# Attention and two feed-forward stages: a second transposition for the upper keys, scatters in pairs, row stores from ScalarE's queue

## The chip, the cores and the metric

The kernel runs on one core of one Trainium2 chip. The metric is the device time of one launch in microseconds; the numbers are medians of runs, and the profile is one execution of its own. TensorE (PE) multiplies matrices and transposes, VectorE (DVE) and ScalarE (ACT) work on elements, GpSimd (POOL) too, and it issues the indirect DMAs; SP only issues DMAs, and ACT issues DMAs besides its own work.

## The reference

```python
# attention, B=8, H=8, S=576, D=64; keys and values are means over 8 neighbours (72 of each)
k_p = k.reshape(B, H, 72, 8, D).mean(axis=3)
v_p = v.reshape(B, H, 72, 8, D).mean(axis=3)
scores = np.matmul(q, k_p.transpose(0, 1, 3, 2)) / np.sqrt(D)
attn = np.exp(scores - scores.max(-1, keepdims=True))
attn_out = np.matmul(attn / (attn.sum(-1, keepdims=True) + 1e-09), v_p)
x = attn_out.transpose(0, 2, 1, 3).reshape(4608, 512)
# one of eight experts for each row, by the largest of eight gate values
e_idx = np.argmax(x @ w_gate + modality_bias[modality_id], axis=1)
out[mask] = gate_w[mask, None] * (np.maximum(x[mask] @ w1[e], 0.0) @ w2[e])
# a second feed-forward stage over all rows
h = out @ w_in
solu = h * softmax(h)
y = (layer_norm(solu) * g_ln) @ w_out
```

## The kernel before

All matrices are float32. The weights of the feed-forward stages are held as a high and a low part, so that each product is three matmuls (lines 735 to 737).

**Attention** fills the first 200 us or so. The 64 pairs of batch and head are worked on batch by batch. The keys and the values of a batch are 8 heads x 72 pooled rows = 576 rows, in five row blocks of 128, 128, 128, 120 and 72 rows (`ROWS`). For each block `load_kv` loads a tile `kc` of keys and one `vc` of values (L267). `kv_a` (L328) pools them: the keys by a VectorE reduction (`pool_k`, L302) into `kv[:, 0]`, the values into `kv[:, 1]`, for the first 19 blocks on VectorE (L340), for the others by three additions on GpSimd (L345 to L347). `kv_b` (L353) transposes `kv`, keys and values side by side, in one TensorE transposition for each block (L359): the keys come out on partitions 0 to 63 and the values on 64 to 127. `kv_e` (L362) copies them out of PSUM on ScalarE: the keys into `kb[0:64, 0]` (L369), the values into `vt` (L372).

The scores of two rows of queries are made in one matmul: `kb` has the keys twice, once in its lower partitions and plane 0, once in the upper partitions and plane 1, since the query tile holds one query row in each half. For the first batch `first_keys` (L306) writes both halves; for the others the upper half comes by a DMA from the lower half, L371, on ScalarE's queue, once for a batch when its last block is there. `kv_c` and `kv_d` multiply the pooled values with the gate's weights and build `vb`, whose columns are the values and the gate's share of them (L383, L396, L399).

A **unit** is up to 256 query rows of one batch, or the last 64 rows of two batches; there are 20. For a unit `st_q` transposes queries (L422), the scores are made (L452 for the shared units, L456), VectorE takes a maximum (L466), ScalarE the exponentials (L490), TensorE transposes them back (L503, L506), ScalarE copies them (L516, L518), and `st_v` multiplies them with `vb` (L545). `st_w` (L553) then divides by the sum on VectorE, makes the row block `xr` of 128 rows (L570) and the gate's values (L573, L576), and stores the rows to `xs` in DRAM by a DMA on SP (L577), 36 in all.

Nine row blocks at a time are **routed**: `route` finds the expert, `rank` (L607) counts each row's place in its expert's list with small matmuls (L617, L619), and `scatter` (L632) writes each row's place, weight and token into the list `perm` by an indirect DMA on GpSimd, one for each of the nine blocks (L640). When 18 blocks have been written, `choose` (L664) takes the expert with the most rows; its weights are loaded, its list is read and its rows are gathered from `xs` (L702), as the first slot of the feed-forward part. The table `FIRST` says how many steps after the choice each of these comes.

The order of the work is written as a list of parts, `ORDER`, which each step runs through with lags in units; a scheduler then sets each engine's order. In a step "a" is `kv_a`, "b" `kv_b`, "k" `kv_e`, "c" `kv_c`, "d" `kv_d`, "w" `st_w`, "r" `rank` and "z" `scatter`. After attention come the decoding of `w_in` and `w_out` and, from 307 us, the slots of 256 rows.

Of the kernel before, what the change touches and what calls it, by code (L numbers as in the profile page):

```python
# [37 lines left out]
# which groups of a unit's scores have their maximum taken off on VectorE  # L38
SUBG = ((2,),) * 20
# after which of the first values the second unit's queries are loaded  # L40
# [3 lines left out]
# the row blocks (five to a batch) whose values are pooled on VectorE, not GpSimd  # L44
# [3 lines left out]
# the first slot's loads, by steps since its expert was chosen  # L48
FIRST = {
    1: (("1", 0),),  # L50
    2: (("i", 0), ("g", 0), ("s", 0)),
# [3 lines left out]
    6: (("t", 0),),  # L55
# [3 lines left out]
# a step's parts: what, which, and how many units ahead of the step  # L59
# [9 lines left out]
# the last pair's tiles that are routed together  # L69
# [10 lines left out]
def chunk_attention_moe_solu_kernel(  # L80
# [79 lines left out]
    def fixed_load(src, n, i, *_):  # L160
        kk, cc = divmod(i, n // 512)
        # before the first slot's exponentials their place serves too
        in_ec = (i if n > 512 else 8 + i) in EC
        st = ec_p.tile([128, FF], F32, name="ec") if in_ec else stg_p.tile([128, 1024], F32, name="stg")
        rows = src[128 * kk:128 * kk + 128, 512 * cc:512 * cc + 512]
        if src.dtype != I64:
            SY.dma_start(out=st[:, 0:512], in_=rows)
        else:
            SY.dma_start(out=st.bitcast(I32), in_=rows.bitcast(I32))
        return st  # L170

    def fixed_chunk(st, src, n, i, hi, lo, scale=None):
        """Chunk i (512 columns) of a [rows, n] weight, rows 128 to a partition block, as hi + lo."""
# [6 lines left out]
        else:  # L180
# [5 lines left out]
            # the high word read as a float32 orders magnitudes too: below float32's range they become 0  # L186
# [24 lines left out]
    def expert_load(src, e, kk, n):  # L211
        """Rows of expert e's weight for n of its row blocks of 128, 1024 floats to a partition."""
        st = stg_p.tile([128, 1024], F32, name="stg")
        SY.dma_start(
            out=st.rearrange("p (k f) -> p k f", k=n),
            in_=src[bass.ds(e, 1), 128 * kk:128 * (kk + n), :].rearrange("a (k p) f -> p (a k) f", p=128))
        return st
# [6 lines left out]
    def behind(op, other):  # L224
        """Keeps op behind an earlier one of its engine."""
        tc.add_manual_dep(op.ins, other.ins.name, mybir.DependencyInfo(mybir.DependencyClass.NoSync, mybir.DependencyReason.DATA))
# [71 lines left out]
    # a batch's pooled keys and values in three groups of its five row blocks  # L298
# [7 lines left out]
    def first_keys():  # L306
        """The first batch's pooled keys, ahead of its values."""
# [7 lines left out]
        for b, cs in KG[:3]:  # L315
            a0, z0 = ROWS[cs[0]][0], ROWS[cs[-1]][1]
            kt = pstr.tile([128, 512], F32, name="tr")
            for c in cs:
                a, z = ROWS[c]
                kv = kx_p.tile([128, 2, D], F32, name="kv")  # L320
                pool_k(kv, k_t.pop((b, c)), z - a)
                PE.transpose(out=kt[0:64, a - a0:z - a0], in_=kv[:z - a, 0], identity=ident[:z - a, :z - a])
                PE.matmul(out=kt[64:128, a - a0:z - a0], lhsT=kv[:z - a, 0], rhs=ident[:z - a, :z - a], start=True, stop=True)
                kv_0.append(kv)
# [3 lines left out]
    def kv_a(i):  # L328
        b, cs = KG[i]
        kv_st[i] = []  # L330
        for c in cs:
            n = ROWS[c][1] - ROWS[c][0]
            vc = v_t.pop((b, c))
            if b == 0:
                kv = kv_0[c]
            else:
                kv = kx_p.tile([128, 2, D], F32, name="kv")
                pool_k(kv, k_t.pop((b, c)), n)
            if 5 * b + c in VD:
# [8 lines left out]
            if b == 0 and op is not None:  # L348
                # the keys are waited for first
                behind(op, kv_last[-1])  # L350
            kv_st[i].append(kv)

    def kv_b(i):  # L353
# [3 lines left out]
        for c, kv in zip(cs, kv_st[i]):  # L357
            a, z = ROWS[c]
            PE.transpose(out=kt[:, a - a0:z - a0], in_=kv[:z - a].rearrange("p a d -> p (a d)"), identity=ident[:z - a, :z - a])  # L359
        kv_kt[i] = kt  # L360

    def kv_e(i):  # L362
# [7 lines left out]
        if b and cs[-1] == 4:  # L370
            ACT.dma_start(out=kb[64:128, 1, :], in_=kb[0:64, 0, :])  # L371
# [31 lines left out]
    # units: five per pair of batches (b, k0) (b, k1) (the last 64 tokens of both) (b+1, k0) (b+1, k1)  # L403
# [27 lines left out]
    # scores of a unit in three banks of (up to) six blocks of 72: block i is head i//n of row r = i%n  # L431
    # (in the unit of two batches' ends: head i)
# [89 lines left out]
    def group(i):  # L522
        """The tiles that are routed together: a pair of batches' nine, of the last pair five and four."""
# [4 lines left out]
    # heads' 73 columns follow each other over two banks: seven of them end at the first one's end  # L528
    def st_v(u, r):
# [5 lines left out]
        if not ps2 and s_done.get(NU - 1) == 3 and not any(x[0] == "s" for x in ps):  # L535
            # no more scores: their banks hold every other tile of the last units
# [16 lines left out]
    def st_w(u, r):  # L553
# [23 lines left out]
        SY.dma_start(out=xs[128 * i:128 * i + 128, :], in_=x)  # L577
# [29 lines left out]
    def rank():  # L607
# [8 lines left out]
        # row p of tile j: earlier rows of its tile, and all of the tiles before it  # L616
# [10 lines left out]
        DVE.tensor_copy(out=pi[:, 0:n], in_=pf[:, 0:n])  # L627
        pending.append([g0, pi, n, 0])

    pending = []  # L630

    def scatter(now=False):  # L632
        if not pending:
            return
        if pending[0][3] < 0 and not now:
            pending[0][3] += 1
            return
        g0, pi, n, _ = pending.pop(0)
        for j in range(n):
# [16 lines left out]
    def pick_first(dst, val, tmp, mx):  # L656
        """dst = one-hot of the first largest of val, over the last axis of 8."""
# [6 lines left out]
    def choose():  # L664
        """The expert with most tokens so far, of 18 tiles, has more than SLOT: its first two slots go first."""
# [48 lines left out]
    def take(pool, shape, dt, name):  # L714
        """A tile: a new one, or, in the last slot's two branches, the next of those that both hold."""
# [40 lines left out]
    # the first slot's first stages go between the last units' parts  # L756
# [45 lines left out]
    def more_loads():  # L802
# [14 lines left out]
        # a row's place in xs and its token  # L817
# [31 lines left out]
    for it in range(IT0, NU - min(lag for _, _, lag in ORDER)):  # L849
# [20 lines left out]
        if first is None and len(scatters) >= 18:  # L870
            choose()
            first = it
        for op, x in FIRST.get(it - first, ()) if first is not None else ():
            if op == "i":
                ids0 = id_p.tile([128, 2, 3], I32, name="ids")
# [56 lines left out]
    def tables(tp):  # L932
# [23 lines left out]
        # the expert that goes last: the one with fewest rows in its last slot  # L956
# [35 lines left out]
        # rows left from a slot's start; its first row; its expert (an empty slot has the first one's)  # L992
# [68 lines left out]
    def st_S(s, t, pf):  # L1061
        """Off with the mean; the sum of squares."""
# [7 lines left out]
    def st_R(s, t, n):  # L1070
        """Rows' scale: r / sqrt(r^2 mean(c^2) + 1e-6) with r = 1 / (sum + 1e-9)."""
# [7 lines left out]
        # 1 / sqrt: a first value from the bits, then Newton's steps  # L1079
# [51 lines left out]
    def switch_regs(s):  # L1131
        """Whether slot s needs another expert's weights, which, and its first row."""
# [16 lines left out]
    def switch_split(ce, sts, dh, dl, n, pool=(), after=()):  # L1149
        with tc.If(ce[0] == 1):  # L1150
            for i in range(4):
                ops = expert_split(sts[i], flat(dh[:, n * i:n * i + n]), flat(dl[:, n * i:n * i + n]), POO if i in pool else DVE)
                if i == 0:
                    # behind what the tensor engine waits for
# [22 lines left out]
    for s in range(NSTAT - 1):  # L1177
# [8 lines left out]
        if s > 1:  # L1186
            # behind what the tensor engine waits for
# [209 lines left out]
```

## Time and profile before

| what | value |
| --- | --- |
| median of 3 runs | 1095.69 us |
| lowest and highest run | 1093.2 and 1097.76 us |
| span of the profiled execution | 1114.2 us |
| mean granted TensorE clock in it | 0.981 |
| TensorE busy | 1060.4 us (95%) |
| VectorE busy | 573.9 us (52%) |
| ScalarE busy | 403.9 us (36%) |
| GpSimd busy | 218.2 us (20%) |

No time of the profiled execution other than its span is recorded. The shares are means over stages with different limits, so they are to be read by stage. A duration of a matmul in the rows is from its issue to its modelled end, and successive ones overlap.

### The profile page before, as it was taken

To read this page: it belongs to the slowest core of one execution; us is meant where nothing else is said; L and a number is where in the kernel's file an instruction comes from. 1 tells how busy PE (TensorE), PEld (TensorE's weight loads), DVE (VectorE), ACT (ScalarE), POOL (GpSimd) and SP (SyncE) were. 2 spreads that over 40 slices of the span, in tenths; PEclk is the share of its full clock that TensorE was granted. 3 is DMA by queue.
4 is the path that set the end of the run, shared out by engine and by line. 5 is a ranking of instruction groups with operands and counts; after the bars stand their busy time and mean duration, and the time that the engine had idled before them with its cause. 6 is when DMAs were issued, how large, how long until landed. Compare 5 with 4: busy or idle time off the path is not lost.

```text
span 1114.2 us, 18506 instructions
## 1 busy us (share of the span) xinstructions
PE 1060.4 (95%) x6961; PEld 963.0 (86%) x6961; DVE 573.9 (52%) x1460; ACT 403.9 (36%) x870; POOL 218.2 (20%) x284
## 2 busy tenths in 40 slices
PE   5898979789999999999999999999999999999997
PEld 4788868788889899898998989999898998989875
DVE  7986757899953434333444433434335343333254
ACT  3666657444522322222234222322234222222232
POOL 3147453453420101101013010100121011010001
PEclk8999989989999999999999999999999999999999
DMA  9887856332200101001033010101221010010000
GB/s 254 222 243 216 242 170 213 107 115 96 77 30 11 38 1 39 29 11 39 1 115 100 15 39 2 37 8 32 97 93 39 1 39 26 8 39 2 19 19 32
DMA packets 58960, 81.19 MB, mean 73 GB/s; under 512 B 16670, under 2 KB 33054, under 8 KB 58848
## 3 DMA queue, kind: packets, MB, share of 16 engines
q1 hardware_dynamic: 50608, 59.28, 17.7%
q0 software_dynamic: 7152, 19.46, 5.1%
q10 hardware_dynamic: 1088, 1.05, 0.4%
q8 instruction: 59, 0.97, 0.4%
q14 instruction: 53, 0.43, 0.1%
HBM read 59.37 MB, written 19.63 MB: 71 GB/s over the span
## 4 chain that ended last, share of the span: by engine, by line
PE 62%; issue 10%; DVE 1%; POOL 1%; another core or an unknown queue 0%; POOLq 0%; ACT 0%
PE ab L736 15%; PE ab L735 15%; PE ab L737 15%; PE h L736 5%; PE h L735 5%; PE h L737 5%; PE tr L1101 2%; PE tr L728 1%; POOL out_dram L1120 1%; DVE ta L208 0%; DVE hl L752 0%; DVE ec L1067 0%; DVE ec L1054 0%; DVE c L1077 0%
## 5 line engine op out<-in xcount | busy, mean ns | idle before, releaser
L1120 POOL DMA_INDIRECT out_dram<-o,ids x37 | 37.7, 1019 | 683.0 <-ACT o L1119 557.9
L735 PE MATMUL ab<-hh,w2h 128*128 128x256 f32 x576 | 165.9, 288 | 3.7 <-DVE rpf L626 3.7
L737 PE MATMUL ab<-hh,w2l 128*128 128x256 f32 x576 | 163.7, 284 | 0.0
L736 PE MATMUL ab<-hl,w2h 128*128 128x256 f32 x576 | 163.2, 283 | 0.5 <-DVE hl L752 0.5
L735 PE MATMUL ab<-xh,w1h 128*128 128x256 f32 x544 | 154.6, 284 | 2.9 <-DVE hl L752 1.8
L736 PE MATMUL ab<-xl,w1h 128*128 128x256 f32 x544 | 154.3, 284 | 0.0
L737 PE MATMUL ab<-xh,w1l 128*128 128x256 f32 x544 | 153.5, 282 | 0.0
L736 PE MATMUL h<-wil,yh 128*128 128x512 f32 x296 | 116.4, 393 | 1.9 <-POOL wil L202 1.9
L735 PE MATMUL h<-wih,yh 128*128 128x512 f32 x296 | 117.9, 398 | 0.1
L737 PE MATMUL h<-wih,yl 128*128 128x512 f32 x296 | 116.0, 392 | 0.0
L735 PEld LDWEIGHTS ab<-hh,w2h 128*128 128x128 f32 x576 | 109.9, 191 | 3.8 <-issue 3.8
L736 PEld LDWEIGHTS ab<-hl,w2h 128*128 128x128 f32 x576 | 110.0, 191 | 0.7 <-DVE hl L752 0.7
L737 PEld LDWEIGHTS ab<-hh,w2l 128*128 128x128 f32 x576 | 109.1, 189 | 0.0
L1053 ACT ACTIVATE ec<-h,c,ids 128x1024 f32<-128x1024 f32 x36 | 43.4, 1207 | 177.4 <-DVE c L1052 177.3
L735 PEld LDWEIGHTS ab<-xh,w1h 128*128 128x128 f32 x544 | 102.5, 188 | 4.4 <-DVE hl L752 2.0
L737 PEld LDWEIGHTS ab<-xh,w1l 128*128 128x128 f32 x544 | 104.0, 191 | 0.0
L736 PEld LDWEIGHTS ab<-xl,w1h 128*128 128x128 f32 x544 | 102.8, 189 | 0.8
L1051 DVE TENSOR_REDUCE c<-h 128x1 f32<-128x1024 f32 x37 | 45.3, 1224 | 111.2 <-PE h L737 111.2
L735 PE MATMUL ab<-woh,ch 128*128 128x512 f32 x256 | 99.7, 389 | 0.0
L737 PE MATMUL ab<-woh,cl 128*128 128x512 f32 x256 | 99.6, 389 | 0.0
L736 PE MATMUL ab<-wol,ch 128*128 128x512 f32 x256 | 99.6, 389 | 0.0
L752 DVE SCALAR_TENSOR_TENSOR hl<-ab,hh 128x512 fp32r<-128x512 f32 x68 | 46.9, 689 | 98.2 <-ACT hh L751 98.2
(279 smaller groups left out, 2048.2 us busy)
## 6 DMA issues: line engine op xcount, KB each, us to landing
stg<-in_moe_w_dram SPq DMA_DIRECT2D x24, 512.0 KB
xs<-xr SPq DMA_DIRECT2D x36, 256.0 KB
qc<-in_q_dram SPq DMA_DIRECT2D x16, 512.0 KB
kc<-in_k_dram SPq DMA_DIRECT2D x24, 256.0 KB
vc<-in_v_dram SPq DMA_DIRECT2D x24, 256.0 KB
stg<-in_moe_w_in_dram SPq DMA_DIRECT2D x4, 512.0 KB
ec<-in_moe_w_in_dram SPq DMA_DIRECT2D x4, 512.0 KB
ec<-in_moe_w_out_dram SPq DMA_DIRECT2D x4, 512.0 KB
```

Of the source, the lines that this page charges most:

```text
L728: PE.transpose(out=p[:, kk, :], in_=x[:, 128 * kk:128 * kk + 128], identity=ident)
L735: PE.matmul(out=o, lhsT=hi, rhs=rhi, start=first, stop=False)
L736: PE.matmul(out=o, lhsT=hi, rhs=rlo, start=False, stop=False)
L737: PE.matmul(out=o, lhsT=lo, rhs=rhi, start=False, stop=last)
L752: b = DVE.scalar_tensor_tensor(out=hl[:, m:m + 2], in0=p, scalar=0.0, in1=hh[:, m:m + 2].bitcast(F32), op0=ALU.max, op1=ALU.subtract)
L1051: DVE.tensor_reduce(out=mx[:, c1], in_=pf, axis=AX.X, op=ALU.max)
L1053: ACT.activation(out=ec, in_=pf, func=ACTF.Exp, bias=nb[:, c1], scale=g[:, c1], accum_out=s1[:, c1])
L1101: PE.transpose(out=p[:, j, :], in_=c[:, f:f + 128], identity=ident)
L1120: sc = POO.indirect_dma_start(out=out, out_offset=bass.IndirectOffsetOnAxis(ap=d["tok"][t], axis=0), in_=o, in_offset=None, bounds_check=N ...
```

## The change

1. **Keys.** The pooled tile `kv` gets a third plane. For the batches after the first, GpSimd copies the pooled keys into it (a new line, 339 in the changed file), so that planes 0 and 1 are keys and values and planes 1 and 2 values and keys. `kv_b` transposes both pairs, into columns 0 to 255 and 256 to 511 of its PSUM tile: the second has the keys on partitions 64 to 127. `kv_e` copies them from there into the upper half of `kb` on ScalarE. The DMA of L371 is gone.
2. **Scatters.** `scatter` gives out at most two of a group's nine in a step (all that are left after the last step). `choose` runs when 18 blocks have been ranked instead of scattered; of the first slot, the load of its list ("i") and the gather ("g") stand six steps behind the choice instead of two.
3. **Stores.** `st_w` stores its rows to `xs` from ScalarE's queue instead of SP's.

```diff
 FIRST = {
     1: (("1", 0),),
-    2: (("i", 0), ("g", 0), ("s", 0)),
+    2: (("s", 0),),
     3: (("s", 1),),
     4: (("s", 2),),
     5: (("s", 3), ("2", 0)),
-    6: (("t", 0),),
+    6: (("i", 0), ("g", 0), ("t", 0)),
...
@@ kv_a
-                kv = kx_p.tile([128, 2, D], F32, name="kv")
+                kv = kx_p.tile([128, 3, D], F32, name="kv")
                 pool_k(kv, k_t.pop((b, c)), n)
+                POO.tensor_copy(out=kv[:n, 2], in_=kv[:n, 0])
...
@@ kv_b
-            PE.transpose(out=kt[:, a - a0:z - a0], in_=kv[:z - a].rearrange("p a d -> p (a d)"), identity=ident[:z - a, :z - a])
+            for j in range(2 if b else 1):
+                PE.transpose(
+                    out=kt[:, 256 * j + a - a0:256 * j + z - a0], in_=kv[:z - a, j:j + 2].rearrange("p a d -> p (a d)"),
+                    identity=ident[:z - a, :z - a])
...
@@ kv_e
         if b:
             ACT.copy(out=kb[0:64, 0, a:z], in_=kt[0:64, 0:z - a])
-        if b and cs[-1] == 4:
-            ACT.dma_start(out=kb[64:128, 1, :], in_=kb[0:64, 0, :])
+            ACT.copy(out=kb[64:128, 1, a:z], in_=kt[64:128, 256:256 + z - a])
...
@@ st_w
-        SY.dma_start(out=xs[128 * i:128 * i + 128, :], in_=x)
+        ACT.dma_start(out=xs[128 * i:128 * i + 128, :], in_=x)
...
@@ rank
+        ranked[0] += n
         pending.append([g0, pi, n, 0])
...
@@ scatter
-        if pending[0][3] < 0 and not now:
-            pending[0][3] += 1
-            return
-        g0, pi, n, _ = pending.pop(0)
-        for j in range(n):
+        g0, pi, n, done = pending[0]
+        pending[0][3] = z = n if now else min(n, done + 2)
+        if z == n:
+            pending.pop(0)
+        for j in range(done, z):
...
-        if first is None and len(scatters) >= 18:
+        if first is None and ranked[0] >= 18:
```

In the changed file lines behind 371 stand four further down and those behind the scatters eight or nine. What it does to the engines' orders is shown at three places.

**GpSimd, the first run of scatters.** Before (L345 to L347 are the values' three additions, L640 the scatter, `perm` the list, L399 a part of `vb`):

```order
L345 TENSOR_TENSOR v_1426<-vc 72x256
L346 TENSOR_TENSOR v_1427<-v_1426 72x128
L347 TENSOR_TENSOR kv<-v_1427 72x64
L640 DMA perm<-meta,rpi 36864x3 x9
L345 TENSOR_TENSOR v_1534<-vc 128x256
L399 TENSOR_TENSOR vb_166<-kv,mask 72x64
L346 TENSOR_TENSOR v_1535<-v_1534 128x128
L347 TENSOR_TENSOR kv<-v_1535 128x64
```

The same place in the change (L346 to L348 the additions, L339 the new copy, L648 the scatter):

```order
L348 TENSOR_TENSOR kv<-v_1589 128x64
L339 COPY kv<-kv 128x64
L346 TENSOR_TENSOR v_1719<-vc 128x256
L339 COPY kv<-kv 128x64
L347 TENSOR_TENSOR v_1720<-v_1719 128x128
L648 DMA perm<-meta,rpi 36864x3 x8
L348 TENSOR_TENSOR kv<-v_1720 128x64
L346 TENSOR_TENSOR v_1727<-vc 120x256
L648 DMA perm<-meta,rpi 36864x3
L347 TENSOR_TENSOR v_1728<-v_1727 120x128
L346 TENSOR_TENSOR v_1735<-vc 72x256
```

The nine scatters stood between the last value block of one batch and the first of the next; eight now follow one another within a value block's three additions, later in the order, and the ninth two instructions on.

**ScalarE, where the sixth batch's keys are finished.** Before (L369 and L372 are the copies of keys and values, L371 the DMA, L490 the exponentials, L516 and L518 the copies of transposed exponentials):

```order
L516 COPY eT<-tr 128x512
L369 COPY kb_164<-tr 64x248
L372 COPY vt<-tr 64x248
L518 COPY eT<-tr 72x2x128
L369 COPY kb_164<-tr 64x72
L372 COPY vt<-tr 64x72
L371 DMA kb_164<-kb_164 64x576
L490 ACTIVATE e<-s,nm 128x72 x6
L486 ACTIVATE e<-e 128x2x144
L429 ACTIVATE qT<-tr 128x512
L594 ACTIVATE rex<-ld 128x72
```

The same place in the change (L374 to L376 are the copies, L581 the store, L494 the exponentials, L520 and L522 the copies of transposed exponentials):

```order
L375 COPY kb_164<-tr 64x248
L376 COPY vt<-tr 64x248
L374 COPY kb_164<-tr 64x72
L375 COPY kb_164<-tr 64x72
L376 COPY vt<-tr 64x72
L494 ACTIVATE e<-s,nm 128x72 x6
L490 ACTIVATE e<-e 128x2x144
L581 DMA xs<-xr 128x512
L433 ACTIVATE qT<-tr 128x512
L520 COPY eT<-tr 128x512
L494 ACTIVATE e<-s,nm 128x72 x3
L598 ACTIVATE rex<-ld 128x72
```

The DMA of the keys is gone, each copy of keys has a second beside it, and a store of rows stands ahead of the copies and exponentials that follow it.

**SP, in the middle of attention's loads.** Before (L267 loads keys or values, L285 queries, L577 stores rows):

```order
L285 DMA qc<-in_q_dram 128x8x128
L267 DMA kc<-in_k_dram 72x512
L267 DMA vc<-in_v_dram 72x512
L577 DMA xs<-xr 128x512 x2
L267 DMA kc<-in_k_dram 128x512
L267 DMA vc<-in_v_dram 128x512
L267 DMA kc<-in_k_dram 128x512
L267 DMA vc<-in_v_dram 128x512
L285 DMA qc<-in_q_dram 128x8x128
L577 DMA xs<-xr 128x512 x2
```

The same place in the change:

```order
L285 DMA qc<-in_q_dram 128x8x128
L267 DMA kc<-in_k_dram 72x512
L267 DMA vc<-in_v_dram 72x512
L267 DMA kc<-in_k_dram 128x512
L267 DMA vc<-in_v_dram 128x512
L267 DMA kc<-in_k_dram 128x512
L267 DMA vc<-in_v_dram 128x512
L267 DMA kc<-in_k_dram 128x512
L267 DMA vc<-in_v_dram 128x512
L285 DMA qc<-in_q_dram 128x8x128
```

The loads follow one another, without stores between them.

## Rows read from the trace of the kernel before

**Rows 1.** The page's first line.

```profile
span 1114.2 us, 18506 instructions
```

**Rows 2.** Busy time by 28-us windows: engines with instructions (x), granted clock, DMA share, GB/s.

```profile
55.00:83.00 28.00, 25.89 (x198) 23.16 (x195) 24.33 (x68) 18.59 (x63) 11.75 (x25) 1.00 0.82 243
...
139.00:167.00 28.00, 22.23 (x151) 19.52 (x150) 14.53 (x48) 16.37 (x57) 14.78 (x26) 0.88 0.56 169
...
167.00:195.00 28.00, 25.64 (x190) 22.75 (x189) 21.40 (x64) 22.29 (x62) 10.18 (x9) 0.94 0.69 214
...
307.00:335.00 28.00, 28.00 (x152) 24.20 (x152) 13.58 (x28) 7.54 (x13) 5.99 (x6) 1.00 0.09 30
```

**Rows 3.** TensorE's waits to 310 us: line, releaser, total us, times, longest.

```profile
PE tr L422 <- DMA qc<-in_q_dram: 6.0, 2, 4.3
...
PE tr L503 <- DVE vb L396: 5.5, 1, 5.5
...
PE s L452 <- DMA kb<-kb: 3.5, 2, 2.6
...
PE av L545 <- issue: 3.1, 1, 3.1
...
PE s L456 <- DMA kb<-kb: 1.9, 1, 1.9
```

**Rows 4.** TensorE's timeline: start, duration, line, operation, count, [idle before <-releaser].

```profile
125.85 1.28 PE L452 MATMUL s<-kb,qT 128*64 128x144 f32 x10 [2.60 <-DMA kb<-kb]
...
160.91 0.38 PE L359 MATMUL tr<-ident,kv 128*128 128x128 f32 x2
...
164.36 0.60 PE L503 MATMUL tr<-ident,e 128*128 128x128 f32 x4
...
165.12 1.58 PE L545 MATMUL av<-vb,eT 128*128 128x146 f32 x10
...
173.77 0.46 PE L452 MATMUL s<-kb,qT 128*64 128x144 f32 x2 [0.88 <-DMA kb<-kb]
...
174.16 3.13 PE L545 MATMUL av<-vb,eT 128*128 128x146 f32 x10
```

**Rows 5.** The columns of rows 2, in two short windows.

```profile
126.30:129.70 3.40, 3.40 (x19) 2.30 (x14) 2.06 (x7) 1.86 (x6) 1.34 (x4) 0.50 0.90 307
...
174.10:177.50 3.40, 3.40 (x14) 3.10 (x14) 0.81 (x5) 1.10 (x3) 1.14 (x1) 0.50 0.80 287
```

**Rows 6.** Groups by line and shape, 27 to 200 us: busy us, mean ns, idle before.

```profile
L347 POOL TENSOR_TENSOR kv<-v 128x64 f32<-128x64 f32 x12 | 3.8, 319 | 0.9
...
L369 ACT COPY kb<-tr 64x248 f32<-64x248 f32 x7 | 2.5, 363 | 3.7 <-PE tr L359 2.5 <-PE tr L506 1.2
...
L369 ACT COPY kb<-tr 64x256 f32<-64x256 f32 x6 | 2.2, 374 | 1.1 <-PE tr L359 1.1
...
L369 ACT COPY kb<-tr 64x72 f32<-64x72 f32 x7 | 1.5, 213 | 0.0
```

**Rows 7.** Issues of L371 and L577: ns min/median/max, first and last start.

```profile
L371 ACTq DMA_DIRECT2D kb<-kb x7: 468/468/519, 34.4 to 169.8; - x7
...
L577 SPq DMA_DIRECT2D xs<-xr x36: 319/344/1817, 46.7 to 213.2; - x36
```

**Rows 8.** SP's queue, waits to 230 us, columns as in rows 3.

```profile
SPq L577 <- DVE lt L573: 25.1, 10, 7.3
```

**Rows 9.** GpSimd's timeline at the second run of scatters.

```profile
134.76 1.01 POOL L640 DMA_INDIRECT perm<-meta,rpi  x1 [6.88 <-DVE rpi L627]
...
136.07 0.96 POOL L640 DMA_INDIRECT perm<-meta,rpi  x1 [0.30 <-issue]
```

**Rows 10.** TensorE's timeline at that run's end and at the first slot's rows.

```profile
148.23 0.66 PE L503 MATMUL tr<-ident,e 128*128 128x128 f32 x2 [5.49 <-DVE vb L396]
...
203.88 1.15 PE L728 MATMUL tr<-ident,x 128*128 128x128 f32 x8
```

**Rows 11.** GpSimd's timeline at the first slot's gather.

```profile
173.49 1.74 POOL L702 DMA_INDIRECT x<-xs,ids  x1 [0.30 <-issue]
```

More of the change, by code (lines that the diff above doesn't have):

```diff
@@ L336, in kv_a @@
             else:
-                kv = kx_p.tile([128, 2, D], F32, name="kv")
+                kv = kx_p.tile([128, 3, D], F32, name="kv")
                 pool_k(kv, k_t.pop((b, c)), n)
+                POO.tensor_copy(out=kv[:n, 2], in_=kv[:n, 0])
             if 5 * b + c in VD:
@@ L627, in rank @@
         DVE.tensor_copy(out=pi[:, 0:n], in_=pf[:, 0:n])
+        ranked[0] += n
         pending.append([g0, pi, n, 0])
     pending = []
+    ranked = [0]
     def scatter(now=False):
@@ L874, in chunk_attention_moe_solu_kernel @@
             if op == "i":
+                assert len(scatters) >= 18
                 ids0 = id_p.tile([128, 2, 3], I32, name="ids")
```

## The prediction

> **What bounds the kernel.** I read the page's first lines, then the busy time by 28-us windows, then TensorE's waits, then the timeline around each wait, and last the queues. The profiled execution spans 1114.2 us [rows 1]; the median of the runs is 1095.69 us, 18.5 us less, so a wait in the trace may be larger than in the runs. I make the sum as a difference and apply it to the median. The windows show two regimes [rows 2]: from 307 us on TensorE is busy all 28 us of a window, and nothing of this change is executed there; in the attention stage it has 2 to 6 us of 28 to spare, at a granted clock of 0.88 to 1.00. So only TensorE's idle and half-speed time in the first 223 us can be won. In the three attention windows shown ScalarE is busy 16 to 22 of 28 us and GpSimd 10 to 15. The list of TensorE's waits [rows 3] shows two kinds that the change can reach. The first is the keys' copy to the upper partitions by DMA: 3.5 us in two waits at L452 and 1.9 us at L456. The second are the long ones, 5.5 us behind the values with the gate's columns (L396) and 3.1 us of "issue", both late in a run of scatters on GpSimd.
>
> **Part 1: keys by a second transposition.** Removed are seven DMAs (L371) from ScalarE's queue and the waits on them. Three of the seven are waited for, 1.9 us at L456 [rows 3] and 2.60 and 0.88 us at L452 [rows 4], together 5.4 us. Behind the second and the third stands a stretch of 3.4 us at a granted clock of 0.50, the lower of the two levels (1.2 against 2.4 GHz), where the windows just read all busy [rows 5]; ten L545 matmuls take 3.13 us in the second of them and 1.58 us at full clock [rows 4]. TensorE had waited before both. If both stretches go, 3.4 us x 0.5 x 2 = 3.4 us come back. They need not go: the other waits stay. Gain 5.4 to 8.8 us at most, and I take 8.8, since the idle time ahead of the two stretches is mainly these waits.
>
> Added on TensorE are 35 transpositions (seven batches, five row blocks). Four 128x128 transpositions take 0.60 us and two take 0.38 us [rows 4], so one more costs (0.60 - 0.38)/2 = 0.11 us: 35 x 0.11 = 3.9 us. The blocks of 120 and 72 rows are a little shorter; I take 3.7 us. This lies wholly on the path, for TensorE has no cover in these windows but the idle time counted above.
>
> Added on ScalarE are 21 copies, seven each of the durations 374, 363 and 213 ns [rows 6]: 7 x 0.95 = 6.7 us. Removed are seven issues of 0.468 us, 3.3 us [rows 7]. Added on GpSimd are 35 copies of 64 columns; the nearest row is a 64-column addition at 319 ns [rows 6], so 11.2 us. What hides them is GpSimd's own idle time, 13 us and more in each window [rows 2]; without that cover up to 11.2 us would follow, because the second transposition now waits for that copy where the first waited for the pooled keys and values alone. Where this copy comes late is within the runs of scatters (part 3). I take 0.
>
> **Part 2: stores of xs from ScalarE's queue.** Thirty-six issues leave SP and come to ScalarE. On SP one is 0.344 us [rows 7], 12.4 us in all, but what SP loses is the waiting: it stood 25.1 us at these stores, in ten waits, for VectorE's L573 alone [rows 8], and the loads of keys, values and queries stood behind. Yet the only load that TensorE waits for in this stage is the queries', 6.0 us in two waits [rows 3], and both lie ahead of the first store at 46.7 us [rows 7], so earlier loads are worth 0; if SP's lead ran out, a wait of the size of a kept DMA wait (1.9 to 2.6 us) could show, or one of them vanish. On ScalarE a DMA issue costs 0.468 us [rows 7], so 16.8 us. With the copies and less the seven issues ScalarE has 16.8 + 6.7 - 3.3 = 20.2 us more to do in about 170 us. In the three attention windows it has 6 to 12 us of 28 free [rows 2], and the added work is 20.2 x 28/170 = 3.3 us a window, so on average it fits. But what stands behind each store in ScalarE's order are exponentials and the copies of transposed scores that TensorE wants next. Bounds: 0, if all falls into ScalarE's idle time, and 20.2 us, if all is on the path. Nearest is the row of ScalarE's free time, so I take a tenth, 2.0 us. The Trainium skill ("Perfetto Trace Analysis", section "DMA Instruction — HWDGE") says that the generator of descriptors is locked for one issuing engine at a time and is shared. By that rule ScalarE's store would also wait for a load that SP is just issuing, and my 2.0 us would be a little more, perhaps 2.2 us as an estimate. The row of the seven issues on ScalarE has 468 ns as minimum and 519 ns as maximum, so no long lock was met in this trace and I keep 0.468 us.
>
> **Part 3: scatters two a step.** The text of the change gives out two scatters a step. The order of GpSimd's instructions in the change shows something else: runs of eight with one behind, again eight and one, then two, the first slot's gather, and thirteen; before, the runs were nine, nine and seventeen. So eight still follow one another. One scatter takes 1.3 us from start to start (134.76 to 136.07) [rows 9], so a run shrinks from about 11.7 to 10.4 us. TensorE's stall of 5.49 us ends at 148.23 [rows 10], so it began at 142.7 us, 8 us after that run's first scatter. Eight are long enough for it: in this part the change doesn't do what it says. I take 0 gain, with the whole 3.1 + 5.5 us as the other bound. The first slot's list and gather move from two steps behind the choice to six. The second half of its gather was issued at 173.49 us [rows 11], and the first transposition of these rows ran at 203.88 us [rows 10]: 30 us of cover. Twenty units in about 170 us make a step some 8.5 us, and four steps would take all; but the choice itself comes one step earlier, so 5 us are left. If that cover is gone, TensorE's transposition waits by some us, but it has attention work of the last pair to do; I take 0.
>
> **The sum.** -5.4 - 3.4 + 3.7 + 2.0 = -3.1 us, and 1095.69 - 3.1 = **1092.6 us**. That is within 0.5% (5.5 us), about what a measurement of this kernel can tell from no change.
>
> **Rival 1: the scatters' stalls end too.** If a run of nine is what makes the engines stop, or the next steps' work now stands ready beside it, the waits of 3.1 and 5.5 us go [rows 3], and what half-clock follows them. For this speaks that the stall begins only when most of a run is through [rows 9, 10]. Against it speaks the order with its eights, and the profiled execution's surplus of 18.5 us over the median: the stalls may be smaller in the runs, and then there is less to win. With 8.6 us, and up to 5 us more of clock, it gives 1079 to 1084 us.
>
> **Rival 2, on the other side: ScalarE's queue blocks.** A store on ScalarE waits until VectorE has made its row block, and all that is behind it waits too. On SP such waits at L577 come to some 50 us by all the rows of the list that name VectorE's attention work, of which the largest stands here [rows 8]: 1.4 us for each of 36. A window of 28 us has six stores; at 0.47 + 1.4 us each, and 1.1 us for copies, that is 12.3 us against 9.4 us of free time in the window from 55 us [rows 2]. So it decides from a mean wait of about 0.9 us a store: below, ScalarE still has room; at 1.4 us there are 2.9 us too much in each of six windows, 17 us. With -8.8 + 3.7 + 17 = +12 the time is 1107 us. For it speaks ScalarE's 22.29 busy of 28 us in the window from 167 us [rows 2]; against it, that SP met its stores early because it had nothing else to do, while ScalarE comes to them later. The Trainium skill ("Perfetto Trace Analysis", section "DMA Instruction — HWDGE") has the wait for semaphores on the issuing sequencer, outside the profiled issue; the rows agree, with 344 ns for an issue [rows 7] beside 25.1 us of waits [rows 8].
>
> **How the numbers follow.** My forecast has 0.56: 0.36 within the band, 0.17 below 1090.2 us (ScalarE's 2.0 us falling away and half a stretch at the lower clock beyond the two are enough) and 0.03 above 1101.2 us. Rival 1 has 0.24, rival 2 has 0.20. So faster 0.17 + 0.24 = 0.41, same 0.36, slower 0.03 + 0.20 = 0.23. The range 1080 to 1104 us leaves out the lower part of rival 1 and the upper half of rival 2, and takes in the bounds of ScalarE's and GpSimd's costs; the forecast's own range is 1087 to 1098 us.
>
> **What would show it.** Right: no wait on a keys' DMA at L452 and L456; transpositions of keys and values doubled at 0.11 us each; ScalarE's busy time up by about 6.7 us of copies and its queue by 36 issues of near 0.47 us; scatters in runs of eight with the stall before their end still there. Wrong: waits of TensorE on exponentials or on copies of transposed scores that grow by over 5 us (rival 2), or the stalls beside the scatters gone (rival 1). A wait of TensorE for the first slot's rows would show that I missed the moved gather.

## The result and the profile after

The changed kernel takes 1104.31 us in the median of 12 runs (1102.9 to 1109.17), the kernel before 1097.14 us in 12 runs beside it (1093.2 to 1101.24). The ratio is 1.0064, with a 95% interval of 1.0048 to 1.0079: slower by some 7 us, where 1092.6 us was forecast.

The profiled execution of the change spans 1107.5 us, less than the 1114.2 us of [rows 1]. Its time was 1109.17 us, so what lies around a span is 1.7 us. By that the execution behind the rows of the prediction took about 1115.9 us, and none of the 12 runs of the kernel before did. The profiled execution of the change is also the longest of its 12, 4.9 us over their median. The first line of the changed kernel's page, then its windows (columns as in [rows 2]):

```profile
span 1107.5 us, 18644 instructions
```

```profile
55.00:83.00 28.00, 27.94 (x219) 25.42 (x218) 26.61 (x69) 20.95 (x73) 14.82 (x35) 1.00 0.93 276
...
139.00:167.00 28.00, 25.64 (x185) 23.29 (x184) 18.78 (x59) 19.92 (x62) 7.61 (x16) 0.94 0.70 204
...
195.00:223.00 28.00, 18.73 (x133) 18.42 (x133) 22.27 (x69) 7.67 (x15) 17.48 (x19) 0.82 0.19 40
```

Against [rows 2] TensorE is busy 2.1 us more from 55 to 83 us and 3.4 us more from 139 to 167 us. In the window from 195 us it idles 9.3 us, at a granted clock of 0.82. TensorE's waits to 320 us (columns as in [rows 3]) have no keys' DMA any more. At the top stands a wait for the first slot's second half (`ab` is its output); the kernel before has it too, with 3.1 us in its second profile below:

```profile
PE ab L743 <- DVE base L628: 7.5, 1, 7.5
```

**The kernel before, profiled again** (the first run of the experiments), is the fairer partner. It spans 1094.0 us. Its windows lack the holes of [rows 2], and of the keys' waits 4.2 us are left (page, windows, TensorE's waits). Against it the change is not denser throughout: TensorE is busy 0.8 us more from 55 to 83 us and 1.3 us less from 139 to 167 us.

```profile
span 1094.0 us, 18506 instructions
```

```profile
55.00:83.00 28.00, 27.15 (x207) 24.24 (x206) 25.52 (x71) 19.67 (x68) 11.70 (x25) 1.00 0.76 229
...
139.00:167.00 28.00, 26.89 (x201) 24.17 (x200) 22.34 (x67) 23.88 (x74) 12.27 (x23) 1.00 0.74 237
```

```profile
PE s L456 <- DMA kb<-kb: 2.7, 2, 2.2
...
PE s L452 <- DMA kb<-kb: 1.5, 1, 1.5
```

Where do the two traces part? TensorE's timeline at the first slot, of the kernel before (second profile) and of the change: the transposition of its rows, its first matmul with w1, its first with w2.

```profile
184.12 1.14 PE L728 MATMUL tr<-ident,x 128*128 128x128 f32 x8
...
186.49 0.36 PE L735 MATMUL tr<-xh,w1h 128*128 128x256 f32 x1
...
203.02 0.36 PE L735 MATMUL ab<-hh,w2h 128*128 128x256 f32 x1 [3.11 <-DVE rpf L626]
```

```profile
188.32 0.60 PE L736 MATMUL tr<-ident,x 128*128 128x128 f32 x4
...
192.74 0.36 PE L743 MATMUL tr<-xh,w1h 128*128 128x256 f32 x1
...
216.38 0.55 PE L743 MATMUL ab<-hh,w2h 128*128 128x256 f32 x1 [7.50 <-DVE base L628]
```

The lag is 4.2 us at the rows, 6.3 us at w1 and 13.4 us at w2. From there to the span's end it is 891.0 us before and 891.1 us after. So between these two executions all of the loss is made ahead of the first slot's second half, and more than half of it between w1 and w2. They are 13.5 us apart and the medians 7.2 us, so the lags show where the loss lies and not how large it is in most runs.

**What TensorE waits for there.** The second half needs four relu's of ScalarE (`hh`, L759; L751 before). ScalarE's timeline in the change:

```profile
207.43 0.68 ACT L187 ACTIVATE ta<-stg 128x512 f32<-128x512 f32 x1 [3.87 <-POOL wil L202]
208.01 0.60 ACT L197 CAST wih<-ta 128x512 fp32r<-128x512 f32 x1
208.52 0.59 ACT L759 ACTIVATE hh<-tr 128x512 fp32r<-128x512 f32 x1
213.23 0.66 ACT L187 ACTIVATE ta<-ec 128x512 f32<-128x512 f32 x1 [4.12 <-POOL wil L202]
213.80 0.61 ACT L197 CAST wih<-ta 128x512 fp32r<-128x512 f32 x1
214.31 0.59 ACT L759 ACTIVATE hh<-tr 128x512 fp32r<-128x512 f32 x1
```

The row of the wait names VectorE's L628. Just ahead of it VectorE makes the low part of the last relu (L760), so TensorE may have waited for either; both follow the last relu, which ends at 214.90 us:

```profile
215.55 0.68 DVE L760 SCALAR_TENSOR_TENSOR hl<-tr,hh 128x512 fp32r<-128x512 f32 x1
...
216.15 0.15 DVE L628 TENSOR_TENSOR base<-base,tr 128x8 f32<-128x8 f32 x1
```

Both late relu's stand behind a decoding step of `w_in` (L187) that waits until GpSimd has finished an earlier chunk (L202), and GpSimd's L202 stand between late scatters:

```profile
206.10 1.29 POOL L202 TENSOR_TENSOR wil<-ta,tb 128x512 fp32r<-128x512 f32 x1
207.56 0.98 POOL L648 DMA_INDIRECT perm<-meta,rpi  x1 [0.17 <-issue]
208.85 1.35 POOL L648 DMA_INDIRECT perm<-meta,rpi  x1 [0.30 <-PE tr L623]
...
211.60 1.60 POOL L202 TENSOR_TENSOR wil<-ta,tb 128x512 fp32r<-128x512 f32 x1
```

The order of ScalarE's instructions in this place shows why. Before:

```
L751 ACTIVATE hh<-tr 128x512
L187 ACTIVATE ta<-stg 128x512
L751 ACTIVATE hh<-tr 128x512
L187 ACTIVATE ta<-ec 128x512
L197 CAST wih<-ta 128x512
...
L751 ACTIVATE hh<-tr 128x512
L187 ACTIVATE ta<-stg 128x512
L197 CAST wih<-ta 128x512
L751 ACTIVATE hh<-tr 128x512
```

In the change the two relu's of the timeline above are the last two of the four, and each stands behind a step of L187 and L197.

Before, one relu stands behind a step that waits for GpSimd, now two do. No line of the change touches this place; the scheduler set it anew. That the loads of `w_in` on SP no longer stand behind the last stores can be a reason, but not the only one: the keys' part alone, with all stores on SP, has a changed order there as well. I call the order of the engines from attention's end on the later order.

**The first slot's rows** come 4.2 us later for another reason. GpSimd's timeline, and SP's issue of the list's load:

```profile
173.57 1.75 POOL L648 DMA_INDIRECT perm<-meta,rpi  x1 [24.72 <-DMA xs<-xr]
175.63 0.96 POOL L648 DMA_INDIRECT perm<-meta,rpi  x1 [0.30 <-issue]
183.75 0.98 POOL L710 DMA_INDIRECT x<-xs,ids  x1 [7.17 <-DMA ids<-perm]
```

```profile
181.35 0.35 SPq L885 DMA_DIRECT2D ids<-perm  x1
```

The list's load is issued after the scatters that were written ahead of it. Six steps behind the choice these are 20 and not 18, and the last two belong to the third group, which starts only at 173.6 us. So the gather stood at 183.75 us, 4.6 us ahead of the transposition, and GpSimd, which keeps its order, stood 7.17 us for the list with eleven scatters and the decoding behind it.

### The profile page after: what moved, and what is told of

Same layout as the page of the kernel before. It is cut to its first block, busy times and chain, and to the rows that moved or that the text cites. A ratio compares the mean times of both kernels' runs of the same rounds, so it can differ in the third digit from the quotient of the medians.

```text
span 1107.5 us, 18644 instructions
## 1 busy us (share of the span) xinstructions
PE 1062.1 (96%) x6996; PEld 967.1 (87%) x6996; DVE 572.1 (52%) x1460; ACT 409.4 (37%) x891; POOL 225.5 (20%) x319
## 5 line engine op out<-in xcount | busy, mean ns | idle before, releaser
L760 DVE SCALAR_TENSOR_TENSOR hl<-ab,hh 128x512 fp32r<-128x512 f32 x68 | 46.9, 689 | 98.3 <-ACT hh L759 98.3
```

The lines of the kernel that those rows point to most:

```text
L760: b = DVE.scalar_tensor_tensor(out=hl[:, m:m + 2], in0=p, scalar=0.0, in1=hh[:, m:m + 2].bitcast(F32), op0=ALU.max, op1=ALU.subtract)
```

## The experiments

Eighteen runs in five groups; the kernels of a group share a chip and the runs of the kernel before. In the first three groups that one took 1095.68 to 1097.82 us, in the last two 1116.21 and 1117.0 us. The prediction's median, and the result, belong to the lower level; its rows belong to the upper one.

**Group 1: each part alone, and the kernel before again.** Edits: of the change's three parts two are undone. Undone, the keys, the stores and the scatters read, one under the other:

```diff
-                POO.tensor_copy(out=kv[:n, 2], in_=kv[:n, 0])
...
-            for j in range(2 if b else 1):
...
+            PE.transpose(out=kt[:, a - a0:z - a0], in_=kv[:z - a, 0:2].rearrange("p a d -> p (a d)"), identity=ident[:z - a, :z - a])
...
-            ACT.copy(out=kb[64:128, 1, a:z], in_=kt[64:128, 256:256 + z - a])
+        if b and cs[-1] == 4:
+            ACT.dma_start(out=kb[64:128, 1, :], in_=kb[0:64, 0, :])
...
-        ACT.dma_start(out=xs[128 * i:128 * i + 128, :], in_=x)
+        SY.dma_start(out=xs[128 * i:128 * i + 128, :], in_=x)
...
-        pending[0][3] = z = n if now else min(n, done + 2)
+        pending[0][3] = z = n
...
-        if first is None and ranked[0] >= 18:
+        if first is None and len(scatters) >= 18:
```

With the scatters the list's load and the gather go back to two steps behind the choice.

> The kernel before, once more, for a second trace. If the stalls beside the scatter runs belong to the program, its span is near 1114 us and TensorE waits 3 to 5 us late in both runs of nine again; if they were a disturbance of the one profiled execution, the span is near the median of the runs, 1097 to 1101 us, and those waits are gone or small.

> The keys' second transposition alone, with the stores on SP and nine scatters a step. Theory A (ScalarE's queue is what makes the change slower): this part gains, ratio 0.995 to 0.998, by 5.4 us of waits less 3.7 us of transpositions. Rival B (the keys' part itself costs, by 35 transpositions and the copies on GpSimd): ratio 1.002 to 1.007. Rival C (the late scatters and gather cost): ratio 0.995 to 1.000 here.

> The stores on ScalarE's queue alone. Theory A: ratio 1.006 to 1.012, with waits of ScalarE at the stores and of TensorE on exponentials or transposed copies. Rivals B and C: ratio 0.998 to 1.002.

> The scatters two a step, with the choice by ranked blocks and the first slot's list and gather four steps later, alone. Theory A and rival B: ratio 0.998 to 1.002. Rival C: ratio 1.004 to 1.010, with a wait of TensorE at the first slot's rows or just behind attention.

| run | ratio (95%) |
| --- | --- |
| kernel before again | one run, 1095.81 us |
| keys alone | 1.0059 (1.0039 to 1.0080) |
| stores alone | 1.0269 (1.0245 to 1.0293) |
| scatters alone | 1.0132 (1.0106 to 1.0158) |

Each part alone is slower, the stores and the scatters by more than any range that was given, and their sum is far above the change. The stores alone show one reason why they can't be added: the keys' DMA shares ScalarE's queue with the stores there, and TensorE's waits for it rise from 4.2 to 13.3 us.

```profile
PE s L457 <- DMA kb<-kb: 9.5, 3, 4.4
...
PE s L453 <- DMA kb<-kb: 3.8, 1, 3.8
```

Two traces say more. With the keys alone the first slot's rows come at 185.3 us and its second half at 203.9 us, against 184.1 and 203.0 us in the kernel before; from there to the end it is 897.2 us instead of 891.0. So 6.2 of the 7.1 us between these spans lie in the later order, and attention gains nothing from the keys' part in this execution. With the scatters alone the order of TensorE, VectorE, ScalarE and GpSimd is, from the place at 186 us of the kernel before to the end, the same as there, and still the run is 1.3% slower; why was not found.

**Group 2: the change without one part, and the list one step earlier.** The first three undo one part each; the fourth is

```diff
-    5: (("s", 3), ("2", 0)),
-    6: (("i", 0), ("g", 0), ("t", 0)),
+    5: (("i", 0), ("g", 0), ("s", 3), ("2", 0)),
+    6: (("t", 0),),
```

> The change without its part 3: the second transposition and the stores on ScalarE's queue, scatters nine a step as before. Alone these parts gave 1.006 and 1.027. Theory A (the stores cost because the keys' DMA stands behind them on one queue, and part 1 takes that DMA away): ratio 1.000 to 1.007. Rival B (ScalarE's queue costs by itself): ratio 1.025 to 1.035.

> The change without its part 2: the second transposition and the scatters two a step, stores on SP as before. Alone these parts gave 1.006 and 1.013. Theory A with independent parts 1 and 3: ratio 1.016 to 1.022, well over the change's 1.006, as then the stores on ScalarE must be what gains within the change. Rival B (the stores cost by themselves): ratio below 1.000.

> The change without its part 1: stores on ScalarE's queue and scatters two a step, the keys' upper copy by DMA as before. Theory A: the wait on the keys' DMA stays, ratio 1.025 to 1.045, and TensorE waits over 10 us for that DMA. Rival B: ratio 1.010 to 1.020.

> The change with the first slot's list and gather five steps behind the choice instead of six. At six, the list's load waits for two scatters of the third group of nine, which are ranked only at 173 us in the changed kernel's trace. If that wait is on the path, as the first slot's weights' matmuls begin 6 us later than before, the ratio falls to 1.001 to 1.004; if the tail is held by the late scatters themselves (they keep GpSimd from the decoding), it stays at 1.005 to 1.008.

| run | ratio (95%) |
| --- | --- |
| without the scatters' part | 1.0057 (1.0036 to 1.0078) |
| without the stores' part | 1.0046 (1.0029 to 1.0063) |
| without the keys' part | 1.0237 (1.0208 to 1.0267) |
| list at five steps | 1.0046 (1.0031 to 1.0061) |

The second transposition takes away what the stores cost through the keys' DMA: without it the change stands at 1.0237, and TensorE waits 15.3 us for that DMA. Both theories for the run without the stores fall: independent parts were to give 1.016 to 1.022, stores that cost by themselves a ratio below 1.000, and 1.0046 was measured. All its stores are on SP and its later order is, on the same four engines, that of the kernel before, so the stores and the new order together account for some 0.2% of the change's 0.64%, between two groups and with intervals that overlap. The list at five steps gains 0.18%, within the two intervals' width; a part of the loss, not most.

**Group 3: one store decides the later order.** The last stores go by SP again:

```diff
-        ACT.dma_start(out=xs[128 * i:128 * i + 128, :], in_=x)
+        (ACT if i < 29 else SY).dma_start(out=xs[128 * i:128 * i + 128, :], in_=x)
```

With 29 TensorE's order from attention's last transpositions to the end is, row for row, that of the kernel before; with 30 it is not. The third run has 29 and the list at five steps, the fourth 30 with scatters nine a step, where the order is the old one from the last of attention on.

> The changed kernel with the stores of the last seven row blocks (29 to 35) on SP again, the first 29 on ScalarE. By this the order of ScalarE's instructions behind attention is the one of the kernel before: the first slot's relu's (L759) stand ahead of the decoding steps (L187, L192, L197) that wait for GpSimd. Theory T (the change loses in the tail, as TensorE waits 7.5 us before the first slot's second half for those relu's, against 3.1 us before): that wait is back to 3 to 4 us and the ratio 0.998 to 1.002. Rival K (the second transposition costs its time in attention and nothing behind it matters): ratio 1.004 to 1.008.

> The same with the last six stores on SP (30 to 35): one store moves, and ScalarE's order behind attention is that of the changed kernel, with the relu's behind decoding steps. Theory T: TensorE's wait before the second half is 6 to 8 us, ratio 1.004 to 1.008. Rival K: the same ratio as with seven, within 0.15%.

> The last seven stores on SP and the first slot's list and gather at five steps. Theory T: 0.995 to 1.000, the best of these. Rival K: 1.003 to 1.006.

> Parts 1 and 2 (scatters nine a step) with the last six stores on SP; here ScalarE's order behind attention is again that of the kernel before. With all stores on ScalarE these parts gave 1.0057. Theory T: 0.998 to 1.002. Rival K: 1.004 to 1.007.

| run | later order | ratio (95%) |
| --- | --- | --- |
| last seven on SP | as before | 1.0043 (1.0020 to 1.0065) |
| last six on SP | new | 1.0101 (1.0079 to 1.0122) |
| last seven, list at 5 | as before | 1.0001 (0.9985 to 1.0017) |
| last six, nine a step | as before | 1.0016 (1.0001 to 1.0030) |

One store moved is worth 0.58%, and TensorE's wait ahead of the second half is 3.8 us with seven and 12.2 us with six, where 6 to 8 us and at most 1.008 were expected (first row of each run's TensorE waits from 165 us; seven, then six):

```profile
PE ab L743 <- DVE rpq L629: 3.8, 1, 3.8
```

```profile
PE ab L743 <- DVE rpq L629: 12.2, 1, 12.2
```

So the later order is shown as a cause, for these two kernels. How much of it is in the change is less clear, for its order is not that with six: against seven, the change itself is 0.2% slower (1.0043 to 1.0064, intervals that overlap), and the seven stores are in that difference. The traces speak for it all the same: from the first matmul with w1 to the first with w2 it takes 13.3 to 20.4 us in the twelve traces with the order as before, and 22.7 to 29.9 us in the six with the order of the change or one near to it (the keys alone and the stores alone have orders of their own).

It is not all: with seven the ratio was to be 0.998 to 1.002. With the list at five steps as well it is 1.0001, so the list costs 0.42% in this order. Little else differs: TensorE and VectorE have the same order from start to end, on GpSimd two scatters stand ahead of the gather instead of behind it, and on ScalarE two stores stand one place off. The first slot's rows come at the same time in both traces (185.5 and 185.7 us). But with the list at six GpSimd stands 7.25 us ahead of the gather, its next L202 ends at 206.6 instead of 201.1 us, the last relu starts at 208.2 instead of 202.7 us, and the second half begins 5.5 us later (208.6 and 203.1 us).

These runs also hold the stores against each other at the lower level: 29 on ScalarE give 1.0043 (last seven on SP), none give 1.0046 (group 2, without the stores' part), both with the list at six steps and the later order as before. No cost of the stores is seen there; the two runs are of two groups.

**Group 4: the parts with the later order as before.** Two, 23 or 14 stores on ScalarE instead of 29; the first two with scatters nine a step, the third with all parts and the list at five.

```diff
-        ACT.dma_start(out=xs[128 * i:128 * i + 128, :], in_=x)
+        (ACT if i < 2 else SY).dma_start(out=xs[128 * i:128 * i + 128, :], in_=x)
```

> The second transposition alone but for the first two stores, which go from ScalarE's queue; the scheduler's order from attention's end on is then that of the kernel before, which it isn't with the transposition alone (1.0059). Theory T (the loss lies in that later order, and the transposition itself gives about what it takes): ratio 0.997 to 1.002. Rival K (the transposition's 35 instructions and copies cost in attention): 1.004 to 1.008.

> The second transposition with the first 23 stores on ScalarE's queue and scatters nine a step; the later order is that of the kernel before. Theory T: 0.996 to 1.002; if the stores on ScalarE cost by themselves beside the transposition, it stands over the run with two stores by 0.002 or more. Rival K: 1.004 to 1.008.

> All three parts with the first 14 stores on ScalarE and the list at five steps; the later order is that of the kernel before. Theory T: within 0.2% of the run with 29 stores on ScalarE (1.0001), so 0.998 to 1.002. If the stores on SP between the loads still cost in attention, it is over 1.002.

| run | ratio (95%) |
| --- | --- |
| keys, two stores | 0.9957 (0.9937 to 0.9977) |
| keys, 23 stores | 1.0015 (1.0000 to 1.0030) |
| all parts, 14 stores, list at 5 | 0.9940 (0.9919 to 0.9961) |

With the later order as before, the second transposition with two stores on ScalarE gains 0.43%, 4.8 us, and 21 more stores cost 0.58%, 6.5 us. The first and the third run lie below the ranges that were expected (from 0.997 and from 0.998), which had been taken from runs at the lower level.

**Group 5: side by side.** The change as it is; the third kernel of group 4; and that one with 2 in the place of 14.

> The changed kernel once more, beside the two that follow, on whatever chip this call gets. Theory T: 1.004 to 1.009 on either chip, with TensorE's wait of 6 us or more before the first slot's second half. If the chip of the last call, where the kernel before took 1116 us, treats the change otherwise, its ratio there is 0.994 to 1.000.

> The three parts with 14 stores on ScalarE and the list at five steps, again. 0.994 was measured where the kernel before took 1116 us. If that gain belongs to the kernel, 0.992 to 0.997 here too; if it belongs to that chip and this call runs where the kernel before takes 1097 us, 0.997 to 1.001.

> The same with two stores on ScalarE. If each store on ScalarE costs some 0.3 us (two against 23 stores gave 0.9957 and 1.0015), 12 fewer are 3 to 4 us less than with 14: a ratio lower by about 0.003. If the stores are free beside the transposition, the same ratio within 0.002.

| run | ratio (95%) |
| --- | --- |
| the change | 1.0061 (1.0037 to 1.0085) |
| all parts, 14 stores, list at 5 | 0.9938 (0.9914 to 0.9962) |
| all parts, two stores, list at 5 | 0.9912 (0.9885 to 0.9939) |

The change costs the same where the kernel before takes 1117 us. But TensorE's wait ahead of the second half, which was to be 6 us or more, is 3.9 us in its trace, as with the list at five steps (3.8 us in group 2); the 7.5 us of the first trace are not what the order always costs.

```profile
PE ab L743 <- DVE base L628: 3.9, 1, 3.9
```

The best version is all parts with two stores on ScalarE and the list at five steps, 1106.3 us against 1117.0 us; there it beats both kernels. It was not run where the kernel before takes 1097 us; the nearest version there, with 29 stores, gives 1.0001. Scatters in pairs with the list at five gain 0.45% at the upper level (0.9957 to 0.9912, in two groups), which is rival 1's direction.

**Where the stores' cost of groups 4 and 5 lies.** The two windows with the holes, in all parts with two stores and then with 14 (group 5):

```profile
83.00:111.00 28.00, 25.68 (x189) 23.77 (x188) 19.46 (x55) 18.40 (x63) 21.38 (x40) 0.94 0.63 171
139.00:167.00 28.00, 25.26 (x180) 22.11 (x179) 22.01 (x59) 22.36 (x70) 8.56 (x21) 0.88 0.81 232
```

```profile
83.00:111.00 28.00, 22.57 (x161) 20.37 (x160) 14.81 (x48) 14.93 (x53) 19.45 (x34) 0.88 0.83 219
139.00:167.00 28.00, 21.90 (x146) 18.34 (x145) 14.82 (x40) 17.00 (x56) 12.25 (x20) 0.88 0.49 147
```

With 14 stores TensorE is busy 6.5 us less in these two windows, where the whole difference is 2.9 us. With the keys and 23 stores instead of two it is busy 43.8 us instead of 50.7 us there, 6.9 us less, where the whole difference is 6.5 us. VectorE and ScalarE are busy 6 to 12 us less in both pairs. So in these traces the cost lies in the stalls beside the runs of scatters, which the lower level does not have, and not in a price of each store.

## Why the prediction was wrong

**What bounds the kernel.** The rows came from an execution of some 1116 us, 20 us above the median that the sum was put on. The prediction saw the surplus but took the rows as a scale. At the median's level, by the second profile, the keys' waits are 4.2 us instead of 5.4 us, no stretch at the lower clock lies behind them, and the stalls of [rows 3, 10] beside the scatters aren't there.

**Part 1: mechanism right, gain mis-sized.** The waits on the keys' DMA are gone. But the 8.8 us were read from the wrong level: by the second profile the same reckoning gives -4.2 + 3.7 = -0.5 us instead of -8.8 + 3.7 = -5.1 us. The trace of the keys alone agrees: it reaches the first slot's rows 1.2 us later than the kernel before, not 5 us earlier. The 4.8 us of group 4 come near the forecast, but at the upper level, and there the stalls are smaller too: TensorE is busy 50.7 us in the two windows with the holes, against 47.1 us in the execution of the prediction's rows, so this is no measurement of the keys' waits alone. The copies on GpSimd take 238 ns, not 319 ns (group by line and shape):

```profile
L339 POOL COPY kv<-kv 128x64 f32<-128x64 f32 x18 | 4.2, 238 | 14.7 <-DVE rs L572 9.3 <-DVE kv L302 5.5
```

**Part 2: 2.0 us stand at the median's level.** With none and with 29 stores on ScalarE the ratio is 1.0046 and 1.0043, so nothing there contradicts the small term. The 6.5 and 2.9 us of groups 4 and 5 lie in the stalls beside the scatters, and why more stores on ScalarE go with longer stalls was not found. The issue is 326 ns, less than the 0.468 us assumed. It does take ScalarE's time: of the 0.41 us of idle time ahead of the next instruction 0.35 are the issue (issues of L581; ScalarE's timeline):

```profile
L581 ACTq DMA_DIRECT2D xs<-xr x36: 326/326/365, 39.0 to 195.3; - x36
```

```profile
72.18 0.35 ACTq L581 DMA_DIRECT2D xs<-xr  x1
72.58 0.95 ACT L494 ACTIVATE e<-s,nm 128x72 f32<-128x72 f32 x4 [0.41 <-DVE lt L577]
```

Rival 2 is not shown: TensorE's waits on exponentials and on copies of transposed scores did not grow by 5 us; to 320 us they come to 3.4 us in the change's trace, 3.1 us more than in the second profile of the kernel before. The lock of the descriptor generator that the Trainium skill describes ("Perfetto Trace Analysis", section "DMA Instruction — HWDGE") does not show in these issues, 326 to 365 ns in 36; leaving it out was right.

**Part 3: the cover was counted wrongly.** The list's move was taken at 0, with 5 us of cover left. The cover was counted in steps up to the rows' transposition, and the rows do come in time. What counted was that the list's load stands behind two scatters of the third group and that GpSimd waits for it ahead of all later scatters and the decoding. It costs 0.42%, 4.6 us, in one group and with nearly all else alike, and 0.18% in the change's order, between two groups. That the scatters stay in runs of eight was right: GpSimd has eight and one behind, twice.

**Missing in the sum: the later order.** The prediction looked at the order up to attention's end, and took nothing of the change to act behind 223 us. The scheduler had moved the first slot's relu's behind decoding steps. Between six and seven stores on SP an order of this kind costs 0.58%, 6.4 us. In the change it is 0.2% with the list at six (1.0043 to 1.0064) and 0.45% with it at five (1.0001 to 1.0046); both differences are between groups and have the last seven stores in them.

**The steps that failed, put together** at the level of the median. All three parts with 29 stores, the list at five and the later order as before give 1.0001, so +0.1 us where the sum says -3.1 us. By the second profile that is the gain of part 1 that wasn't there, which no run at this level tests by itself. The list at six brings this to 1.0043, +4.6 us, where the sum has 0. The last seven stores on ScalarE, and with them the new order, bring it to 1.0064, +2.3 us, which the sum doesn't have.

**Still open.** Why the scatters alone cost 1.3% although the change with the keys and the scatters costs 0.46%. How large the later order is in the change by itself: no run alters the order alone. And what puts the kernel before at 1097 or 1117 us.

## What to carry to other kernels

Where a scheduler sets the order, compare the whole order, not only the lines that the diff touches: one store moved to another queue changed the order behind attention, at a cost of 6 us. Ask of a load which writes stand ahead of it in the program, and what stands behind it on the engine that waits for it, and not only how many steps it moves: two scatters more ahead of it cost 4.6 us. Check that a profile and the median belong to the same level before a wait in it is given a price, and measure the parts at the level at which they are to be used.

## What the runs showed that was not expected

Both kernels take 1.7 to 1.8% longer in the last two groups, and nearly all of the extra time has one place: between the two traces of the change it is 13.2 us, and 12.8 us are in two waits. The changed kernel, profiled there, has these windows and waits of TensorE ("remote": the profile names no instruction of the core that ended the wait):

```profile
83.00:111.00 28.00, 22.37 (x168) 20.34 (x167) 15.55 (x48) 15.22 (x54) 18.34 (x32) 0.88 0.78 219
...
139.00:167.00 28.00, 20.16 (x137) 17.51 (x137) 13.34 (x38) 14.95 (x46) 10.24 (x20) 0.82 0.62 176
```

```profile
PE tr L426 <- remote: 7.5, 1, 7.5
...
PE av L549 <- remote: 5.3, 1, 5.3
```

They are the holes of [rows 2, 3], beside the two runs of scatters, and they are missing in every profile of the first three groups in which the same scatters ran. The number of the chip does not tell the two levels apart: the record has the same one for group 1, where the kernel before takes 1097 us, and for group 4, where it takes 1116 us. What stops the engines while scatters run was not found.
